# Retention with routed feed-forward on one core: a smaller limit on load traffic in the middle of the kernel, and a weight asked for two loads later

## The chip, the cores and the metric

The kernel runs on one core of one Trainium2 chip. The metric is device time in microseconds (us) of one execution, taken as the median over several. A profiled execution gives a trace: when each engine worked, when each transfer was issued and when it landed. The engines are called by the profile's short names: PE (matrix products; PEld is its loading of stationary operands), DVE (vector), ACT (scalar and activation), POOL (here stores, gathers and some vector work) and SP (here nothing but the issuing of loads).

## The reference, cut to what matters

Two blocks follow each other. The first is a retention layer over 8 batches, 8 heads, 576 positions and head size 64:

```python
scores = scale * np.matmul(q, k.transpose(0, 1, 3, 2))
gamma = 1.0 - 2.0 ** (-5.0 - np.arange(H))
rel = pos[:, None] - pos[None, :]
Dmat = np.where(rel >= 0, gamma[:, None, None] ** rel[None, :, :], 0.0)
ret = scores * Dmat[None, :, :, :]
out = np.matmul(ret, v)
```

Its output, as rows of 512, goes through a mixture-of-depths block. In each batch a score picks 128 of the 576 rows; only these pass a two-layer network, are scaled by a gate and added back:

```python
scores = np.einsum('bsd,d->bs', x, w_gate)
top_idx = np.argpartition(-scores[b], capacity)[:capacity]
h = np.maximum(xe @ w1, 0.0)      # w1 is 512 x 1024
ye = h @ w2                       # w2 is 1024 x 512
out[b, top_idx] = x[b, top_idx] + g[:, None] * ye
```

Everything is float32. The kernel is handed q, k, v and a second copy of k.

## The kernel before, in words

The retention is computed in 36 steps, s = 0 to 35 (`NS` = 36, `NC` = 9 in each of 4 groups of two batches). Step s needs one load, "load s": 1 MB in four quarters of 256 KB, which are q and k with the head dimension on the partitions (quarters 0 and 1) and v and k with the positions on the partitions (2 and 3). Steps 0 to 8 are of a wide kind, 9 and 10 of a kind of their own (`first_step`), 11 to 35 of the "pair" kind. The main loop's pass for step s is called slot s here.

In a slot of the pair kind PE first multiplies q and k (`n_open`, tile `sc_ps`, needs quarters 0 and 1 of load s) in turn with the values' product of the step before (`n_values`, tile `y_ps`). Then come one or two pieces of the feed-forward network of batches chosen earlier (`some`, tiles `h_ps` and `ye_ps`), and then the new state (`n_sums`, tile `u_ps`, needs `vs`) in turn with the states' product of the step before (`n_states`). ACT scales v into `vs` for step s + 1 in the middle of slot s (`scaled`, L238), so it needs quarter 2 of load s + 1 then. POOL stores the finished rows.

All loads are issued by SP, in program order, one after the other. Loads 0 to 14 go as halves of 512 KB (`load`), and are put in SP's queue six slots ahead of their step. The first weight w1 goes as four pieces of 512 KB, two ahead of load 10 and two ahead of load 12. These transfers all pass `transfer` (L105), which makes a new one wait until enough earlier ones have landed: what is under way, itself included, stays at or under `most[0]` = 2048 KB.

Loads 15 to 35 go as quarters of 256 KB, taken from a list `later`. `tick` (L152) takes one from the list; it stands at five places of a slot, four with `AHEAD` = 6 and one with 2. It takes nothing when the next load is further ahead of the slot than that; from load 21 on the limit is 3 slots in place of 6, since loads from 21 on share five buffers (`KEPT`) and the ones before have eight. Each quarter waits for the matrix product at whose place it was asked for, but not for earlier transfers' landing by `most`. The second weight w2 stands in the same list, as eight pieces of 256 KB: four behind load 17, four behind load 18. Its first piece is used in slot 19 (`downs`), its fifth at the end of slot 20.

SP's transfers share eight semaphores in turn (DMAHW0 to DMAHW7), so a transfer can also not start before the eighth one ahead of it has landed.

Of the kernel before, what the change touches and what calls it, by code (L numbers as in the profile page):

```python
# [48 lines left out]
def kernel(  # L49
# [16 lines left out]
    nc = tc.nc  # L66
# [5 lines left out]
    NC = NS // NG  # L72
# [30 lines left out]
    most = [2048]  # L103

    def transfer(out, in_, kb):  # L105
        ins = nc.sync.dma_start(out=out, in_=in_)
        behind.append((ins, kb))
        total = 0
        for n in range(len(behind) - 2, -1, -1):
            total += behind[n][1]  # L110
            if total + kb > most[0]:
                tc.add_manual_dep(ins.ins, behind[n][0].ins.name, LANDED, reason="few at once")
                break

    def room(s):
        if s not in raw:
            pool = loads if s > FEWER or s % (KEPT + LENT) < KEPT else lent
            raw[s] = pool.tile([P, 4, DM], F32, name="raw")

    def load(s, a, go=transfer):  # L120
        room(s)
        go(raw[s][:, 2 * a : 2 * a + 2, :], qkvk[s, a], 512)

    def weight(i, go=transfer):

        w, sb = ((w1, w1_sb), (w2, w2_sb))[i // 4]
        n = w.shape[2]
        flat = sb.rearrange("p h a f -> p (h a f)")
        go(flat[:, n * (i % 4) : n * (i % 4) + n], w[i % 4], 512)


    AHEAD, LED = 6, 14
    pe = {"last": None, "slot": 0}
    later = deque()

# [9 lines left out]

    for s in range(LED + 1, NS):
        later.extend((piece, s, a) for a in (2, 3, 0, 1))
        if s in (LED + 3, LED + 4):
            first = 8 if s == LED + 3 else 12
            later.extend((weight_piece, i) for i in range(first, first + 4))  # L150

    def tick(ahead=AHEAD):  # L152
        if pe["slot"] <= NC or not later:
            return
        s = next(a[1] for a in later if a[0] is piece)
        if s > pe["slot"] + (min(ahead, KEPT - 2) if s > FEWER else ahead):
            return
        f, *a = later.popleft()
        out, in_ = f(*a)
        dma = nc.sync.dma_start(out=out, in_=in_)  # L160
        tc.add_manual_dep(dma.ins, pe["last"].ins.name, LANDED, reason="at its moment")

    def mm(out, w, x, start, stop):
# [3 lines left out]
    n_first = col["eye"]  # L167
    load(0, 0)
    transfer(table[:, :n_first], consts[:, :n_first], 139)
    for a in (2, 3):  # L170
        transfer(*piece(0, a), 256)
# [73 lines left out]
    def w_scores(s):  # L245
        for i in range(2):
            sc_ps[s, i] = bank("sc_ps", "mm" if s == FIRST[1] else "sc")
        first = None
        for j, i, h in wide_heads:
            ins = mm(sc_ps[s, i][:, jt[j]], raw[s][halves[i], 1, jt[j]],  # L250
                     raw[s][halves[i], 0, jt[j]], True, True)
            first = first or ins
        return first
# [100 lines left out]
    def in_turn(a, b, moments):  # L354
        for n in range(H):
            for f in (next(a, None), next(a, None), next(b, None), next(b, None)):
                if f:
                    f()
            if n in moments:
                tick(AHEAD if n == 0 else 2)  # L360
# [563 lines left out]
    for g in range(1, NG):  # L924
        s = NC * g + EARLY[g] + 1
# [4 lines left out]
    s = 2 * NC  # L930
# [23 lines left out]
    s = 3 * NC  # L954
# [23 lines left out]
        plan.setdefault((s, 3), []).insert(0, (some, (1,)))  # L978

    def ahead_of(s):  # L980
        if s <= LED:
            load(s, 1)
            load(s, 0)
        if s in (10, 12):
            weight(s - 10)
            weight(s - 9)
# [7 lines left out]
    def first_step(s):  # L994
        if s == FIRST[0]:
            stored(s - 1)
            opened(s + 1)
        else:
            first_sums()
            n_state(s)  # L1000
            tick()
            stored(s - 1)
        do(s, 1)
        tick()
        do(s, 2)
        w_results(s)
        tick()
        values(s)
        do(s, 3)
        tick()  # L1010
# [3 lines left out]
    for s in range(4, AHEAD):  # L1014
        ahead_of(s)
    scaled(0)
    for s in range(NS + 1):
        pe["slot"] = s
        ahead_of(s + AHEAD)
        if s in FIRST:  # L1020
            first_step(s)
# [3 lines left out]
        if wide:  # L1025
            first = w_scores(s)
# [149 lines left out]
```

## Time and profile before

| What | Value |
|---|---|
| median of 3 executions | 247.94 us (245.8 to 249.35) |
| the profiled execution's own time | 247.39 us |
| its span, first to last instruction | 245.6 us |
| PE busy | 227.7 us, 93% of the span |
| DVE busy | 161.4 us, 66% |
| ACT busy | 105.9 us, 43% |
| POOL busy | 52.8 us, 21% |
| moved by DMA | 56.98 MB, mean 232 GB/s |
| SP's loads | 42.67 MB, 49.8% of 16 DMA engines' span |

The page gives the busy time of each engine, then the span in 40 slices of 6.14 us with the busy share of each in tenths, the granted PE clock in tenths of full speed (PEclk) and the share of the DMA engines. A view of windows gives the same for stretches of choice. A timeline row gives the start in us, the duration, the engine, the line and the tiles, and in brackets how long the engine sat idle just before and what ended that; "issue" there means that nothing in the profile ended it. "DMA to landing" is the time from a transfer's issue to its last byte's arrival. The profiled execution's own time is 1.8 us above its span.

### The profile page before, as it was taken

Reading aid. Unit: us, or ns where it says so; the run is one execution under the profiler, and the core shown is the slowest. Engines: PE = TensorE matmul, PEld = TensorE weight load, DVE = VectorE, ACT = ScalarE, POOL = GpSimd, SP = SyncE. Lnnn points to the kernel's source line nnn. Section 1 sums busy time; section 2 is a strip of 40 time slices with the busy share of each in tenths; the row PEclk is TensorE's granted clock in tenths of the full one; section 3 lists DMA queues with packets and bytes.
Section 4 is the critical chain, followed back from the end, with each engine's and each line's share of the span. In section 5 each row is a group of like instructions: output and inputs, shape, how many; then the busy total and the mean of one; then the engine's idle time right before and its main releaser. Section 6 shows DMA issues by size and latency. Waiting matters only on the chain. (4 is left out here: it accounts for less than half of the span.)

```text
span 245.6 us, 10525 instructions
## 1 busy us (share of the span) xinstructions
PE 227.7 (93%) x4587; PEld 188.2 (77%) x4587; DVE 161.4 (66%) x377; ACT 105.9 (43%) x378; POOL 52.8 (21%) x73
## 2 busy tenths in 40 slices
PE   8799999996985999999998999999999999999991
PEld 6598888985975997656556888888899964499880
DVE  3355979893443558979657469987797987173640
ACT  2456574355462654762725445815572140022100
POOL 1442645520200010011602000220002201310011
PEclk9999999998897999999999999999999999999998
DMA  6989999999998789888996578677511210410002
GB/s 216 370 323 405 329 398 410 397 403 378 364 398 288 234 263 306 280 283 272 281 358 241 169 227 280 201 234 265 180 49 71 105 43 0 131 43 3 0 1 85
DMA packets 22974, 56.98 MB, mean 232 GB/s; under 512 B 2960, under 2 KB 3088, under 8 KB 22928
## 3 DMA queue, kind: packets, MB, share of 16 engines
q1 hardware_dynamic: 18720, 42.67, 49.8%
q0 software_dynamic: 4208, 13.64, 15.3%
q8 instruction: 36, 0.59, 1.0%
q14 instruction: 10, 0.08, 0.1%
HBM read 44.76 MB, written 11.53 MB: 229 GB/s over the span
## 5 line engine op out<-in xcount | busy, mean ns | idle before, releaser
L238 ACT ACTIVATE vs<-raw,table 128x64 f32<-128x64 f32 x192 | 48.4, 338 | 1.3 <-DMA raw<-in_qkvk 1.3
L164 PE MATMUL sc_ps<-raw 64*64 64x64 f32 (+1 forms) x976 | 42.2, 235 | 4.0 <-issue 2.8
L164 PEld LDWEIGHTS sc_ps<-raw 64*64 64x64 f32 (+1 forms) x976 | 37.0, 147 | 10.8 <-issue 8.9
L164 PE MATMUL y_ps<-vs,am 64*64 64x64 f32 (+1 forms) x1152 | 42.6, 224 | 1.3 <-DVE am L272 0.7
L164 PE MATMUL h_ps<-xg,w_sb 128*128 128x128 f32 (+1 forms) x256 | 43.1, 318 | 0.3 <-ACT xg L573 0.2
L164 PEld LDWEIGHTS y_ps<-vs,am 64*64 64x64 f32 (+1 forms) x1152 | 37.7, 138 | 2.9 <-DVE am L272 1.4
L164 PE MATMUL ye_ps<-w_sb,hT 128*128 128x512 f32 (+1 forms) x96 | 39.2, 539 | 0.5 <-DVE o L600 0.5
L418 POOL DMA_DIRECT2D out<-xs x25 | 13.9, 556 | 116.6 <-DVE xs L388 116.6
L164 PEld LDWEIGHTS h_ps<-xg,w_sb 128*128 128x128 f32 x256 | 36.2, 198 | 3.5 <-ACT xg L573 0.5
L164 PE MATMUL u_ps<-vs,raw 64*64 64x64 f32 (+1 forms) x864 | 33.2, 224 | 4.2 <-issue 3.5
L164 PEld LDWEIGHTS u_ps<-vs,raw 64*64 64x64 f32 (+1 forms) x864 | 28.6, 137 | 10.3 <-issue 4.3
L388 DVE TENSOR_TENSOR xs<-y_ps,table 128x512 f32<-128x512 f32 x25 | 17.2, 689 | 28.9 <-PE y_ps L164 28.8
L164 PE MATMUL y_ps<-st,raw 64*64 64x64 f32 x736 | 27.8, 224 | 0.3 <-issue 0.3
L517 DVE SCALAR_TENSOR_TENSOR scr<-row,sc,ahead 128x384 f32<-128x384 f32 (+4 forms) x46 | 26.2, 570 | 2.6 <-ACT row L510 1.4
L399 DVE SCALAR_TENSOR_TENSOR scr<-xs,wg 128x512 f32<-128x512 f32 x36 | 26.1, 726 | 1.0
L164 PEld LDWEIGHTS y_ps<-st,raw 64*64 64x64 f32 x736 | 24.1, 137 | 2.7 <-issue 2.4
L164 PEld LDWEIGHTS ye_ps<-w_sb,hT 128*128 128x128 f32 x96 | 16.8, 189 | 10.4 <-issue 8.2
L272 DVE TENSOR_TENSOR am<-sc_ps,table 128x512 f32<-128x512 f32 x22 | 14.2, 685 | 15.3 <-PE sc_ps L164 15.2
L364 DVE TENSOR_TENSOR am<-sc_ps,table 128x512 f32<-128x512 f32 x25 | 17.2, 688 | 8.5 <-PE y_ps L164 6.8
L378 ACT ACTIVATE xs<-y_ps,table 128x64 f32<-128x64 f32 x72 | 15.8, 332 | 8.2 <-PE y_ps L164 8.1
L370 ACT COPY st<-u_ps 128x512 f32<-128x512 f32 x23 | 13.2, 573 | 13.4 <-PE y_ps L164 10.2
L588 ACT ACTIVATE hT<-h_ps 128x128 f32<-128x128 f32 (+1 forms) x20 | 6.8, 340 | 26.6 <-PE h_ps L164 26.6
(113 smaller groups left out, 265.0 us busy)
## 6 DMA issues: line engine op xcount, KB each, us to landing
raw<-in_qkvk SPq DMA_DIRECT2D x86, 256.0 KB, 4.4
raw<-in_qkvk SPq DMA_DIRECT2D x29, 512.0 KB, 6.4
out<-xs POOLq DMA_DIRECT2D x33, 256.0 KB, 4.9
w_sb<-in_w SPq DMA_DIRECT2D x4, 512.0 KB, 6.7
w_sb<-in_w SPq DMA_DIRECT2D x8, 256.0 KB, 6.0
out<-xs POOLq DMA_DIRECT2D x6, 128.0 KB, 5.4
table<-in_consts SPq DMA_DIRECT2D x1, 314.0 KB
wg<-in_w_gate SPq DMA_DIRECT2D x1, 256.0 KB, 5.0
```

What stands on the lines that cost most here:

```text
L164: pe["last"] = nc.tensor.matmul(out, w, x, start=start, stop=stop, skip_group_check=True)
L238: nc.scalar.activation(out=vs[s][:, hd[h]], in_=raw[s][:, 2, hd[h]], func=AF.Copy, scale=by[:, h : h + 1])
L272: nc.vector.tensor_tensor(out=v(am[s][:, i, :]), in0=v(sc_ps[s, i]), in1=mask.unsqueeze(1).to_broadcast([P, HJ, P]), op=OP.mult)
L364: nc.vector.tensor_tensor(out=heads(am[s][:, 0, :]), in0=heads(sc_ps[s]), in1=caus.unsqueeze(1).to_broadcast([P, H, C]), op=OP.mult)
L370: nc.scalar.copy(out=st[s], in_=u_ps[s // NC])
L378: nc.scalar.activation(out=xs[s][:, hd[h]], in_=y_ps[s][:, at : at + D], func=AF.Copy, scale=decw[:, 1, k, h : h + 1])
L388: nc.vector.tensor_tensor(out=heads(xs[s]), in0=heads(y_ps[s]), in1=dec[:, 1, k, :].unsqueeze(2).to_broadcast([P, H, D]), op=OP.mult)
L399: nc.vector.scalar_tensor_tensor(scr, xs[s], 1.0, wg, op0=OP.mult, op1=OP.mult, accum_out=sc["first" if s in FIRST else g][:, k : k + 1])
L418: nc.gpsimd.dma_start(out=outs[2 * g][k], in_=xs[s])
L517: nc.vector.scalar_tensor_tensor(scr[:, : C * (c1 - c0)], row[g][:, C * c0 : C * c1], sc[g][:, c : c + 1], ahead[:, at + C * c0 : at + C * ...
L588: nc.scalar.activation(out=hT[b // 2, i][:, at : at + n, at0 : at0 + w], in_=t, func=AF.Relu)
```

## The change

Three things change. From load 12 on, `most[0]` is 1280 KB in place of 2048 KB. This is set where load 12 and the two w1 pieces ahead of load 13 are put in the queue, so it holds for load 12, these two pieces, and loads 13 and 14. The quarters that `tick` takes go through `transfer` too as long as the next load in the list is 20 or less; before they did not. The w2 pieces stand behind loads 19 and 20 in place of 17 and 18.

```diff
@@ transfer
                 tc.add_manual_dep(ins.ins, behind[n][0].ins.name, LANDED, reason="few at once")
                 break
+        return ins
@@
-    AHEAD, LED = 6, 14
+    AHEAD, LED, LESS = 6, 14, 20
@@
     for s in range(LED + 1, NS):
         later.extend((piece, s, a) for a in (2, 3, 0, 1))
-        if s in (LED + 3, LED + 4):
-            first = 8 if s == LED + 3 else 12
+        if s in (LED + 5, LED + 6):
+            first = 8 if s == LED + 5 else 12
             later.extend((weight_piece, i) for i in range(first, first + 4))
@@ tick
         out, in_ = f(*a)
-        dma = nc.sync.dma_start(out=out, in_=in_)
+        dma = (transfer(out, in_, 256) if s <= LESS else nc.sync.dma_start(out=out, in_=in_))
         tc.add_manual_dep(dma.ins, pe["last"].ins.name, LANDED, reason="at its moment")
@@ ahead_of
+        if s == NC + 3:
+            most[0] = 1280
         if s <= LED:
             load(s, 1)
             load(s, 0)
```

Only SP's queue moves; the order on PE, ACT, DVE and POOL is the same. The first place is SP's queue at load 12 (`raw_509`), the two w1 pieces, load 13 (`raw_580`) and load 14 (`raw_657`), before:

```order
L106 DMA raw_509<-in_qkvk 128x1024 [waits DMAHW2_49,PE_49,Pool_49]
L106 DMA raw_509<-in_qkvk 128x1024 [waits DMAHW3_49]
L106 DMA w1_sb_73<-in_w1 128x1024 [waits DMAHW4_49]
L106 DMA w1_sb_73<-in_w1 128x1024 [waits DMAHW5_49]
L106 DMA raw_580<-in_qkvk 128x1024 [waits DMAHW6_49,PE_49,Pool_49]
L106 DMA raw_580<-in_qkvk 128x1024 [waits DMAHW7_49]
L106 DMA raw_657<-in_qkvk 128x1024 [waits DMAHW0_49,PE_49,Pool_49]
```

The same place after the change:

```order
L106 DMA raw_509<-in_qkvk 128x1024 [waits DMAHW4_49,PE_49,Pool_49]
L106 DMA raw_509<-in_qkvk 128x1024 [waits DMAHW5_49]
L106 DMA w1_sb_73<-in_w1 128x1024 [waits DMAHW6_49]
L106 DMA w1_sb_73<-in_w1 128x1024 [waits DMAHW7_49]
L106 DMA raw_580<-in_qkvk 128x1024 [waits DMAHW0_49,DMAHW2_49,PE_49,Pool_49]
L106 DMA raw_580<-in_qkvk 128x1024 [waits DMAHW3_49,DMAHW1_49]
L106 DMA raw_657<-in_qkvk 128x1024 [waits DMAHW2_49,PE_49,Pool_49]
```

The semaphores are handed out in turn, and the first `raw_509` transfer itself has number 6. So it waited for the fourth transfer ahead of it and now waits for the second: two halves of 512 KB are under way where four were.

The second place is SP's queue around w2 and load 21. The names' numbers rise along the program, so they also tell in which slot a buffer was asked for. Before, from the end of load 17 (`raw_913`) over load 18 (`raw_1129`):

```order
L160 DMA raw_913<-in_qkvk 128x512 [waits DMAHW1_49,PE_49]
L160 DMA w2_sb_74<-in_w2 128x512 [waits DMAHW2_49,PE_49]
L160 DMA w2_sb_74<-in_w2 128x512 [waits DMAHW3_49,PE_49]
L160 DMA w2_sb_74<-in_w2 128x512 [waits DMAHW4_49,PE_49]
L160 DMA w2_sb_74<-in_w2 128x512 [waits DMAHW5_49,PE_49]
L160 DMA raw_1129<-in_qkvk 128x512 [waits DMAHW6_49,PE_49,Pool_49]
```

After, from the end of load 20 (`raw_1358`) over the second half of w2 to load 21 (`raw_1666`):

```order
L106 DMA raw_1358<-in_qkvk 128x512 [waits DMAHW4_49,PE_49]
L161 DMA w2_sb_74<-in_w2 128x512 [waits PE_49] x3
L161 DMA w2_sb_74<-in_w2 128x512 [waits DMAHW5_49,PE_49]
L161 DMA raw_1666<-in_qkvk 128x512 [waits DMAHW6_49,PE_49,Activation_49]
L161 DMA raw_1666<-in_qkvk 128x512 [waits DMAHW7_49,PE_49]
L161 DMA raw_1666<-in_qkvk 128x512 [waits DMAHW0_49,PE_49]
```

Loads 18, 19 and 20 move ahead of pieces of w2, and the second half of w2 now stands directly ahead of load 21. The four pieces behind load 20 already count as "next is load 21", so `tick` takes them at most 3 slots ahead of step 21: in slot 18. Load 21 follows in slot 19, where it was slot 18, and every later load is one slot later than before too. By the names: before, load 21 is `raw_1563` and load 22 `raw_1671`; after, load 21 is `raw_1666`.

## The prediction

> **What bounds the kernel now.** I read the page first, then PE's busy time in windows, then PE's own timeline at the holes, then the DMA view.
>
> ```profile
> PE 227.7 (93%) x4587; PEld 188.2 (77%) x4587; DVE 161.4 (66%) x377; ACT 105.9 (43%) x378; POOL 52.8 (21%) x73
> q8 instruction: 36, 0.59, 1.0%
> ```
>
> PE is the bound: 17.9 us of the span are left to it. The windows (duration; busy time of PE, PEld, DVE, ACT, POOL; granted PE clock; DMA share; GB/s) show where.
>
> ```profile
> 50.00:55.00 5.00, 5.00 (x133) 4.56 (x130) 4.78 (x17) 2.83 (x11) 1.06 (x2) 1.00 1.01 398
> 55.00:60.00 5.00, 3.11 (x77) 2.79 (x78) 2.27 (x4) 2.68 (x10) 0.00 (x0) 0.96 1.02 385
> 60.00:65.00 5.00, 5.00 (x135) 4.55 (x138) 0.72 (x2) 1.23 (x7) 1.57 (x2) 0.70 0.98 343
> 65.00:70.00 5.00, 4.25 (x109) 3.75 (x102) 2.69 (x6) 3.31 (x13) 0.58 (x1) 1.00 1.04 398
> 70.00:75.00 5.00, 3.26 (x128) 2.93 (x127) 2.00 (x5) 2.53 (x10) 0.56 (x1) 1.00 1.05 396
> 75.00:80.00 5.00, 3.50 (x59) 3.26 (x63) 2.00 (x5) 1.69 (x9) 0.00 (x0) 0.67 0.70 253
> 80.00:85.00 5.00, 5.00 (x181) 4.56 (x174) 2.69 (x6) 3.13 (x13) 0.54 (x1) 0.99 0.75 249
> 85.00:90.00 5.00, 5.00 (x137) 4.62 (x137) 2.08 (x4) 3.25 (x13) 0.54 (x1) 1.00 0.84 249
> 160.00:200.00 40.00, 39.67 (x937) 35.98 (x936) 33.47 (x73) 16.24 (x49) 7.19 (x10) 1.00 0.41 136
> ```
>
> Between 55 and 80 us PE has holes, and twice the clock is cut. Up to 75 us the DMA engines are full (share about 1). Behind 80 us PE is busy nearly throughout, at 160 to 200 us 99%, so what is won before 80 us should reach the end. PE's timeline has the holes:
>
> ```profile
> 58.72 0.21 PE L164 MATMUL u_ps<-vs,raw 64*64 64x64 f32 x1 [1.89 <-issue]
> 70.41 0.27 PE L164 MATMUL u_ps<-vs,raw 64*64 64x64 f32 x2 [1.16 <-issue]
> 76.50 0.27 PE L164 MATMUL sc_ps<-raw 64*64 64x64 f32 x2 [2.83 <-issue]
> ```
>
> All three end with "issue", in the middle of a row of equal products whose operands were there: no wait in the profile explains them. Their distance does. The windows between them:
>
> ```profile
> 58.72:70.41 11.69, 10.53 (x255) 9.51 (x255) 4.07 (x8) 6.23 (x24) 2.15 (x3) 0.85 1.01 369
> 70.41:76.50 6.09, 3.26 (x129) 2.93 (x128) 2.00 (x5) 2.12 (x8) 0.56 (x1) 1.00 1.05 395
> ```
>
> PE and PEld together take 510 instructions between the first two and 257 between the last two: twice, and once, about 256. The page's "instruction" queue carries 36 packets of 0.59 MB, and 9174 PE instructions over 36 packets are 255 each. So PE runs out of instructions: the next packet is late, because it travels behind data. The Trainium skill ("Runtime: NRT & Kernel Launch", section "Instruction fetch mechanics") says that instructions come in 16 KiB blocks of 256, which agrees, and that the cost of crossing a block is mostly hidden, which the three holes contradict.
>
> How late a transfer comes goes with how much is under way. Four answers on "DMA to landing" (minimum, median, maximum): the loads issued at 42.9 to 57 us, at 66.2 to 73.6, at 82 to 107, and the one at 79.5.
>
> ```profile
> DMA to landing us min/median/max: 5.8/6.8/7.2
> DMA to landing us min/median/max: 5.6/6.0/7.2
> DMA to landing us min/median/max: 3.2/3.8/4.1
> DMA to landing us min/median/max: 2.9/2.9/2.9
> ```
>
> A quarter alone takes 2.9 us. With 2048 KB under way 6 to 7 us pass, so 3 to 4 us are queue. At 82 to 107 us, where `tick` paces the loads, 3.8 us pass and PE has no hole.
>
> **The change part by part.** *Gaps two and three* (70.41 and 76.50). Here the quarters and w2 go eight at a time, since the eight semaphores let no more through; "none" was 2048 KB in effect. Now it is five quarters. Nothing slower than 3.8 us is to be expected of them: the estimate is 2.9 alone plus the queue of 1280 in place of 2048 KB, less what passes meanwhile, which puts them next to the 82 to 107 us row. Between 70.41 and 76.50 one block needed 6.09 us with landing at 6.0; at 3.8 its fetch would come 2.2 us sooner, 3.9 us. PE's own work in that block is 3.26 us, so a hole of 0.6 remains of 2.83. The two blocks ahead of it needed 10.53 us of work, 5.3 each, above 3.9: the gap of 1.16 goes. Bounds: with landing at 4.8, as the row for 110 to 131 us has it, the remaining hole is 1.6; with 2.9 it is none.
>
> ```profile
> DMA to landing us min/median/max: 3.1/4.8/7.3
> ```
>
> *The clock behind gap three.* The granted clock of 0.67 at 75 to 80 and 0.99 after it costs (1 - 0.67) x 5 + 0.05 = 1.7 us. The gap of 1.16 us drew no cut (1.00 at 70 to 75), so one of 0.6 should not. Saved so far: 1.16 + 2.2 + 1.7 = 5.1 us.
>
> *Gap one and loads 12 to 14.* The hole of 1.89 us and its cut clock (0.04 x 5 + 0.30 x 5 = 1.7 us) could go too, 3.6 us together. But here loads are needed just as they land:
>
> ```profile
> 57.60 2.02 ACT L238 ACTIVATE vs<-raw,table 128x64 f32<-128x64 f32 x8 [1.30 <-DMA raw<-in_qkvk]
> 61.23 0.37 PE L164 MATMUL sc_ps<-raw 64*64 64x64 f32 x2
> 47.34 2.37 SPq L106 DMA_DIRECT2D w_sb<-in_w  x2
> 50.69 5.77 SPq L106 DMA_DIRECT2D raw<-in_qkvk  x4
> ```
>
> ACT waited 1.30 us for load 13's quarter 2. Slot 13 begins at 61.23; without the hole and the 0.8 us of cut clock up to there it would ask for load 13's second half at 58.5. That half was issued at about 52.5 (second of the four from 50.69) and with a median of 6.8 landed at about 59.2: so even without the hole PE would have waited. And the change slows this very load. Two halves may now be under way in place of four. The w1 pieces at 47.34 and 49.4 waited for load 11's halves (four ahead), so these landed then; from 49.4 on the second halves of load 12, w1 and load 13 follow each other, one landing each. A half of 512 KB takes at least what the very first load took:
>
> ```profile
> DMA to landing us min/median/max: 3.7/3.7/3.7
> ```
>
> The other end is 5.6, the quickest of the full stretch. I take 3.9, the near end plus a little for POOL's stores, since two halves seldom fill the engines: 49.4 + 3 x 3.9 = 61.1 us. Slot 13 then begins where it did before (61.23), after a wait of 2.6 us for data in place of 1.89 for instructions, 0.1 won. That wait is long enough to cut the clock (1.89 was), and all 1.7 us of the cut would then follow it, where 0.9 followed before: 0.8 lost. If the wait falls across two of the clock's intervals there is no cut, and 0.9 is won. I put 0.1 for this part, between -0.7 and +1.0; at the earlier pace (59.2) it would be +2.9.
>
> The quarters of load 15 and on stand in SP's queue behind this. There is room: before, SP issued loads 15 to 17 from 56.57 on, and the `u_ps` row at 70.41 is still slot 14. Five per 3.8 us is a load in 3.0 us, against a slot of 4.85 us (four stores, one a slot, between 86.03 and 105.44). So they stay ahead.
>
> ```profile
> 56.57 8.91 SPq L160 DMA_DIRECT2D raw<-in_qkvk  x12
> ...
> 86.03 0.54 POOL L418 DMA_DIRECT2D out<-xs  x1 [3.81 <-DVE xs L388]
> 105.44 0.54 POOL L418 DMA_DIRECT2D out<-xs  x1 [5.67 <-DVE xs L388]
> ```
>
> *w2 later.* Pieces 1 to 4 are asked for in slot 15 and used in slot 19, pieces 5 to 8 in slot 18 and used at the end of slot 20: two slots, 9.7 us, against landings of 3.8. Free; if not, the feed-forward pieces in PE's queue would hold up the retention behind them.
>
> *Loads 21 to 35 one slot later.* Asked for two slots ahead, the last quarter leaves some 2.5 us into the slot and has 9.7 - 2.5 = 7.2 us to land, against a median of 4.8 and a worst case of 7.3; quarter 2 leaves first and has the middle of the next slot, some 7 us. Mostly covered: 0.2 lost, bounds 0 and 1.
>
> Sum: 1.16 + 2.2 + 1.7 + 0.1 - 0.2 = 5.0 us off the profiled execution's own 247.39: 242.4 us. The runs' median is 247.94, half a microsecond above that execution, well inside their 3.5 us of spread; I leave it out.
>
> **The rivals.** *Loads 12 to 14 keep their pace* (A2): the first gap goes as well, 2.9 in place of 0.1, 239.6 us. For it: the bytes ahead of load 13 are the same, and less runs beside them. Against: 512 KB alone takes 3.7 us, and two per 3.7 us are less than the one per 1.7 us at which they passed before (w1 to load 14: 12 transfers from 37.69 to 56.1).
>
> ```profile
> 37.69 1.79 SPq L106 DMA_DIRECT2D w_sb<-in_w  x2
> ```
>
> *The instruction packet's delay does not hang on what SP has under way* (B). If it waits for its turn among full queues whatever stands in them, gaps two and three stay as long as the DMA engines are full, and w2's departure only moves them: 247.4 - 0.1 + 0.2 = about 247.5 us. Against it: with landing at 3.8 us, DMA was still 0.84 full at 85 to 90 us and PE had no hole. The Trainium skill ("DMA: Bandwidth & Descriptors", section "Queues, rings and completion order") speaks for it: each engine goes round its queue rows a packet at a time, so the instruction row should not stand behind all of SP's bytes. Holes of 1 to 3 us in this trace speak against that, as the whole reason at least.
>
> *The limit starves PE at load 13* (C), the slower side. If a half takes 5.6 us even with two under way, load 13 lands at 49.4 + 3 x 5.6 = 66.2, slot 13 begins 5.0 us later than before and the clock takes 0.8; at such landings gap three keeps 2.4 of its 2.83 us and its cut clock, gap two goes: 5.8 - 1.16 - 0.4 + 0.2 = 4.4 us slower, 251.8. It decides from a landing of about 4.9 us on, where load 13 costs 3.8 and the gaps give 4.0. Against it: 3.8 us for quarters at 82 to 107 us with a megabyte under way.
>
> **How the numbers follow.** The forecast 242.4 has 0.50, A2 (239.6) 0.18, B (247.5) 0.20, C (251.8) 0.12. About 2%, 5.0 us, is what a measurement tells from no change; the line is 243.0, just above the forecast. Its own range is 240.5 to 244.5 by the bounds above, and 0.6 of it lies under the line. Faster by over 2%: 0.30 + 0.18 = 0.48. Slower by over 2% (above 252.9): a third of C, 0.04. Within: 0.48. The range leaves out C and the lower tail of A2: 239.3 to 248.2.
>
> **What would show it.** In the changed kernel's profile: no "issue" hole over 1 us at the 256-instruction borders after slot 14, and a clock of 1.00 at 70 to 80 us; loads at 60 to 80 us landing in about 4 us; in place of the first hole a wait of `sc_ps` on `raw` at slot 13, of 1 to 3 us; DMA share under 1 at 50 to 60 us. Wrong would be: holes that stay although landings fall to 4 us (B), a wait at slot 13 of over 4 us (C), or `vs` or `sc_ps` waiting for `raw` beyond slot 21, which would be the lost slot of lead.

## The result and the profile after

The changed kernel takes 251.91 us (median of 20, 249.4 to 255.79) beside 248.25 us for the kernel before (20, 245.51 to 249.84) on the same chip: a ratio of 1.0124, 95% interval 1.0087 to 1.0161. It is slower, where 2% faster was forecast. Ratios here count only executions within 1.5% of the quickest of their kernel, so that one or two quick executions can shift a ratio by 1% against the medians; executions spread over 2 to 3%, and the median of all stands beside each ratio. The profiled execution of the changed kernel, 249.40 us with a span of 247.6, is the quickest of its 20; so it shows less loss than the median has.

The busy times on the page of the changed kernel are those of before to within 1%; the change moved time, not work. (`transfer`'s new line shifts all that follow: L164 is now L165.)

```profile
PE 229.1 (93%) x4587; PEld 189.1 (76%) x4587; DVE 161.2 (65%) x377; ACT 105.9 (43%) x378; POOL 52.8 (21%) x73
q1 hardware_dynamic: 18720, 42.67, 51.6%
```

The same bytes took 51.6% of the DMA engines' span in place of 49.8%. The windows of the changed kernel, with the columns of the prediction's:

```profile
50.00:55.00 5.00, 5.00 (x120) 4.62 (x119) 4.79 (x15) 2.82 (x11) 1.49 (x3) 1.00 0.95 291
55.00:60.00 5.00, 2.93 (x82) 2.52 (x80) 2.81 (x8) 1.72 (x7) 0.55 (x1) 1.00 0.88 291
60.00:65.00 5.00, 3.40 (x70) 3.29 (x71) 0.69 (x1) 1.26 (x6) 1.02 (x1) 0.61 0.94 320
65.00:70.00 5.00, 5.00 (x141) 4.47 (x139) 2.00 (x5) 2.93 (x11) 0.57 (x1) 0.71 0.91 296
70.00:75.00 5.00, 4.68 (x141) 4.19 (x141) 2.69 (x6) 3.50 (x13) 0.56 (x1) 1.00 0.97 309
75.00:80.00 5.00, 4.40 (x127) 3.94 (x128) 3.85 (x9) 2.81 (x14) 0.54 (x1) 1.00 0.97 336
80.00:85.00 5.00, 4.68 (x128) 4.16 (x127) 2.23 (x6) 3.74 (x15) 0.54 (x1) 1.00 0.95 324
85.00:90.00 5.00, 4.79 (x127) 4.40 (x127) 1.95 (x3) 2.86 (x11) 0.30 (x1) 1.00 0.97 342
90.00:95.00 5.00, 3.75 (x134) 3.30 (x128) 3.78 (x11) 2.50 (x11) 0.53 (x2) 1.00 0.90 300
```

Between 50 and 70 us the DMA engines are 0.88 to 0.95 busy, but move 291 to 320 GB/s where before it was 343 to 398. PE stands idle in the middle of it, and two windows of cut clock follow, (0.39 + 0.29) x 5 = 3.4 us. That sum also counts time in which PE was idle: slot 13 itself has 7.21 us of PE's time here, and 4.4 to 4.7 in the four experiments below that pass it at full clock, so the cut cost some 2.5 to 2.8 us. From 70 us on the clock is full and PE has more done per window than before, until about 80; from there to 95 us it has small holes where before had none. PE's timeline of the changed kernel names them:

```profile
61.60 0.37 PE L165 MATMUL sc_ps<-raw 64*64 64x64 f32 x2 [3.67 <-DMA raw<-in_qkvk]
75.44 0.27 PE L165 MATMUL sc_ps<-raw 64*64 64x64 f32 x2 [0.75 <-issue]
80.14 0.27 PE L165 MATMUL y_ps<-vs,am 64*64 64x64 f32 x2 [0.30 <-issue]
85.21 0.27 PE L165 MATMUL row_ps<-table,sc 64*64 64x64 f32 x2 [0.39 <-issue]
90.41 0.27 PE L165 MATMUL sc_ps<-raw 64*64 64x64 f32 x1 [0.29 <-issue]
95.38 0.38 PE L165 MATMUL h_ps<-xg,w_sb 128*128 128x128 f32 x2 [1.33 <-issue]
```

The first is slot 13 waiting for load 13. All the others stand at the borders of instruction packets: PE and PEld together have 2722, 2977, 3232, 3486 and 3741 instructions on record ahead of them, 254 or 255 apart. Up to 100 us holes and cut clock, by windows in both, come to 6.73 + 3.4 = 10.1 us, where before had 5.88 + 3.4 = 9.3. The slots' starts, read from the timelines of the two kernels (us):

| slot | 12 | 13 | 14 | 15 | 16 | 19 | 24 | 35 |
|---|---|---|---|---|---|---|---|---|
| before | 53.74 | 61.23 | 66.37 | 72.59 | 81.61 | 95.56 | 119.65 | 186.27 |
| after | 53.20 | 61.60 | 68.81 | 73.60 | 79.04 | 96.14 | 122.26 | 188.30 |

At slot 14 the changed kernel is 2.4 us behind, at slot 16 it is 2.6 ahead, at slot 19 it is 0.6 behind and at slot 35 2.0, which is the difference of the spans.

SP's timeline of the changed kernel has the halves one by one. Each waits for the landing of the second one ahead of it:

```profile
49.00 0.33 SPq L106 DMA_DIRECT2D w_sb<-in_w  x1
52.13 0.33 SPq L106 DMA_DIRECT2D w_sb<-in_w  x1
54.33 0.33 SPq L106 DMA_DIRECT2D raw<-in_qkvk  x1
57.12 0.33 SPq L106 DMA_DIRECT2D raw<-in_qkvk  x1
58.55 0.33 SPq L106 DMA_DIRECT2D raw<-in_qkvk  x1
61.57 0.33 SPq L106 DMA_DIRECT2D raw<-in_qkvk  x1
```

So the w1 half issued at 49.00 landed by 54.33, after 5.3 us; the next ones took 5.0, 4.2 and 4.5. The last of these is load 13's second half, landed at 61.57, and PE goes on at 61.60. With four halves under way the median was 6.8: half as much under way shortened the landing by 22 to 38% only, and the pace fell by the rest. It had to fall: even at the 3.7 us of a half alone, two halves at a time (1.05 MB) are 283 GB/s, and SP's queue had moved 318 (3.18 MB in 10 us, below). The DMA view shows the pace, and also why a high DMA share misleads. For 50 to 60 us of the changed kernel:

```profile
DMA packets 844, 2.91 MB, mean 291 GB/s; under 512 B 140, under 2 KB 140, under 8 KB 842
q1 hardware_dynamic: 641, 2.34, 76.7%
```

and for 40 to 50 us of before, when the same kind of halves were under way four at a time:

```profile
DMA packets 1124, 4.03 MB, mean 403 GB/s; under 512 B 146, under 2 KB 146, under 8 KB 1122
q1 hardware_dynamic: 874, 3.18, 80.4%
```

SP's queue took 0.767 x 160 / 2.34 = 52 us of engine time per MB after, and 0.804 x 160 / 3.18 = 40 before, 30% more. This is not a load on the engines that the limit made. The kernel before has the same figure at 85 to 106 us, where no limit holds and `tick` paces the loads, 0.733 x 336 / 4.71 = 52:

```profile
DMA packets 2912, 5.84 MB, mean 278 GB/s; under 512 B 352, under 2 KB 352, under 8 KB 2906
q1 hardware_dynamic: 2584, 4.71, 73.3%
```

So a packet's time on the profile is longer where fewer bytes are under way, and a share of 0.84 to 0.95 does not mean that the engines have nothing left: before moves 249 GB/s at 0.84 (85 to 90 us) and 398 at 1.01 (50 to 55).

### The profile page after: what moved, and what is told of

Read it like the earlier page. It is cut to its first block, busy times and chain, and to the rows that moved or that the text cites. A ratio compares the mean times of both kernels' runs of the same rounds, so it can differ in the third digit from the quotient of the medians.

```text
span 247.6 us, 10524 instructions
## 1 busy us (share of the span) xinstructions
PE 229.1 (93%) x4587; PEld 189.1 (76%) x4587; DVE 161.2 (65%) x377; ACT 105.9 (43%) x378; POOL 52.8 (21%) x73
## 3 DMA queue, kind: packets, MB, share of 16 engines
q1 hardware_dynamic: 18720, 42.67, 51.6%
## 5 line engine op out<-in xcount | busy, mean ns | idle before, releaser
L165 PE MATMUL sc_ps<-raw 64*64 64x64 f32 (+1 forms) x976 | 43.6, 236 | 5.6 <-DMA raw<-in_qkvk 4.2
L165 PEld LDWEIGHTS sc_ps<-raw 64*64 64x64 f32 (+1 forms) x976 | 38.0, 148 | 12.3 <-issue 6.4
L165 PE MATMUL y_ps<-vs,am 64*64 64x64 f32 (+1 forms) x1152 | 43.5, 224 | 1.1 <-DVE am L273 0.7
L165 PE MATMUL h_ps<-xg,w_sb 128*128 128x128 f32 (+1 forms) x256 | 42.6, 315 | 1.6 <-issue 1.3
L165 PEld LDWEIGHTS y_ps<-vs,am 64*64 64x64 f32 (+1 forms) x1152 | 38.3, 138 | 3.2 <-DVE am L273 1.4
L165 PE MATMUL ye_ps<-w_sb,hT 128*128 128x512 f32 (+1 forms) x96 | 39.2, 539 | 0.6 <-DVE o L601 0.6
L165 PEld LDWEIGHTS h_ps<-xg,w_sb 128*128 128x128 f32 x256 | 35.9, 196 | 4.9 <-issue 1.4
L165 PEld LDWEIGHTS u_ps<-vs,raw 64*64 64x64 f32 (+1 forms) x864 | 28.6, 138 | 8.1 <-issue 2.3
L165 PE MATMUL u_ps<-vs,raw 64*64 64x64 f32 (+1 forms) x864 | 33.0, 225 | 0.2 <-POOL vs L235 0.2
L165 PE MATMUL y_ps<-st,raw 64*64 64x64 f32 x736 | 28.2, 225 | 1.8 <-issue 1.7
L400 DVE SCALAR_TENSOR_TENSOR scr<-xs,wg 128x512 f32<-128x512 f32 x36 | 27.2, 755 | 1.0
L165 PEld LDWEIGHTS ye_ps<-w_sb,hT 128*128 128x128 f32 x96 | 16.8, 189 | 11.6 <-issue 9.3
L165 PEld LDWEIGHTS y_ps<-st,raw 64*64 64x64 f32 x736 | 24.4, 138 | 1.4 <-issue 1.0
```

The source lines that it names most:

```text
L165: pe["last"] = nc.tensor.matmul(out, w, x, start=start, stop=stop, skip_group_check=True)
L400: nc.vector.scalar_tensor_tensor(scr, xs[s], 1.0, wg, op0=OP.mult, op1=OP.mult, accum_out=sc["first" if s in FIRST else g][:, k : k + 1])
```

## The experiments

Two theories stood first. P (parts) read the loss off the two traces as a sum: 2.4 us by slot 14 (load 13 late, clock cut), 5.0 won by slot 16, 3.2 lost in slots 17 to 19, and 2 from the lead that loads 21 to 35 lose by w2's later place. W (weight): w2's later place does it all. Two more, T and O, came later and are told where they are tested. None of the kernels leaves out any part of the computation.

**The limit without the move of w2.** The change with w2 left behind loads 17 and 18.

```diff
-        if s in (LED + 5, LED + 6):
-            first = 8 if s == LED + 5 else 12
+        if s in (LED + 3, LED + 4):
+            first = 8 if s == LED + 3 else 12
```

> The limit of 1280 KB as in the change, w2 left behind loads 17 and 18. Theory P (parts): the change's 3.7 us are +2.4 by slot 14 (load 13 late, clock cut), -5.0 up to slot 16 (gaps two and three gone), +3.2 in slots 17 to 19 (the backlog of loads, carried more slowly, keeps the instruction packets late for longer) and +2 in slots 21 to 25 (loads 21 to 35 one slot later, by w2's place). Alone, the limit keeps the first three: +0.6 us on before, ratio 1.000 to 1.006. Theory W (w2's place does it all): the limit alone gains what was forecast, 0.980.

Measured: 251.76 us (6 executions, 248.44 to 255.76) beside 247.62, ratio 1.0107 (1.0023 to 1.019). The loss is there without w2's move, so W falls. P's sum falls too: it had 0.6 us of loss without w2's move, and the medians have 4.1. PE's timeline of this kernel, whose profiled execution (251.99 us) is near its median:

```profile
63.82 0.37 PE L165 MATMUL sc_ps<-raw 64*64 64x64 f32 x2 [4.31 <-DMA raw<-in_qkvk]
```

**The move of w2 alone.** Before, with w2 behind loads 19 and 20.

```diff
-        if s in (LED + 3, LED + 4):
-            first = 8 if s == LED + 3 else 12
+        if s in (LED + 5, LED + 6):
+            first = 8 if s == LED + 5 else 12
```

> w2 behind loads 19 and 20, no limit beyond before's 2048 KB. Theory P: only the lost slot of lead remains, +1 to +2 us, 1.004 to 1.008; the hole at 70 us stays, the one at 76 us stays or moves, since the engines are as full. Theory W: the whole loss, 1.012 or more, and more than the change itself has, as the limit's gain is missing.

Measured: 245.83 us (6, one of them far out at 739.93) beside 247.62, ratio 0.9892 (0.9805 to 0.9979). P had expected it to be slower, 1.004 to 1.008, and it is not; whether it is a gain is asked again below.

**The limit on the halves alone.** One line added to before, so that only load 12, two w1 pieces and loads 13 and 14 are held.

```diff
     def ahead_of(s):
+        if s == NC + 3:
+            most[0] = 1280
```

> 1280 KB for the halves alone (load 12, two w1 pieces, loads 13 and 14); quarters and w2 as before. Theory P: the wait of 3 to 4 us at slot 13 and the cut clock come as in the change, +2.4 us by slot 14, and gaps two and three stay, so 1.010. Rival: the wait only takes the place of the first hole and the later ones shrink since SP is further behind: 1.000.

Measured: 252.55 us (6, 250.46 to 256.2) beside 247.62, ratio 1.02 (1.0135 to 1.0265), twice what P had expected. The halves' limit alone costs as much as the whole change, or more. The timeline of its PE, the windows and SP's timeline; the profiled execution was the slowest of its six (256.2 us), so the rows show the mechanism, not its usual size:

```profile
63.72 0.37 PE L164 MATMUL sc_ps<-raw 64*64 64x64 f32 x2 [4.33 <-DMA raw<-in_qkvk]
```

```profile
60.00:65.00 5.00, 1.28 (x48) 1.28 (x52) 0.00 (x0) 2.70 (x11) 0.24 (x1) 0.64 0.87 292
65.00:70.00 5.00, 5.00 (x108) 4.55 (x100) 1.52 (x3) 2.26 (x10) 0.78 (x1) 0.67 0.94 294
```

```profile
47.32 1.73 SPq L106 DMA_DIRECT2D raw<-in_qkvk  x2
51.79 3.18 SPq L106 DMA_DIRECT2D w_sb<-in_w  x2
57.61 6.41 SPq L106 DMA_DIRECT2D raw<-in_qkvk  x4
```

Load 13 leaves SP at 57.61 where it left at 50.69 before. The same wait and the same two windows of cut clock are there as in the changed kernel. (Here and in the kernel without w2's move slot 12 had waited for its load as well, 1.51 and 0.95 us.)

**The limit on the quarters alone.** The change with w2 in its old place and the limit set only after load 14.

```diff
-        if s == NC + 3:
-            most[0] = 1280
         if s <= LED:
             load(s, 1)
             load(s, 0)
+        if s == LED:
+            most[0] = 1280
```

> 1280 KB for the quarters of loads 15 to 20 and w2 (behind loads 17 and 18) alone; halves as before at 2048 KB. Theory P: load 13 as before, gaps two and three smaller (-5.0), later small holes at the 256-instruction borders up to 95 us (+2 to +3): 0.988 to 0.996. Rival, that the late holes eat all of it: 1.000.

Measured: 248.05 us (12 executions) beside 247.62, ratio 0.9988 (0.994 to 1.0036). No gain, as the rival had it. The waits of its PE between 50 and 100 us (total, times, longest):

```profile
PE u_ps L165 <- issue: 2.4, 2, 1.3
PE y_ps L165 <- issue: 2.2, 2, 1.9
PE sc_ps L165 <- issue: 1.2, 1, 1.2
PE h_ps L165 <- issue: 1.1, 1, 1.1
PE row_ps L165 <- issue: 0.7, 1, 0.7
```

Seven smaller holes of 7.5 us in all, up to 94 us, stand in place of before's three of 5.88; the clock is not cut (1.00 in all windows from 55 to 95), which is worth up to 3.4 us against before's profile, and still the time is the same. Its loads issued between 60 and 90 us take 4.8 us to land, by the median:

```profile
DMA to landing us min/median/max: 3.8/4.8/6.2
```

So the limit on the quarters spreads the delay over more borders instead of taking it away. This execution is 0.5 us ahead of before's at slot 19 (95.06 for 95.56), level at slot 24 and behind from a hole of 1.41 at 123.99 on.

**The move of w2 with the lead kept.** The kernel with only w2 moved, and besides `tick` takes a w2 piece one slot earlier, so that loads 21 to 35 keep their lead of 3.

```diff
+        if later[0][0] is weight_piece:
+            s -= 1
```

> x2_weight_alone with w2's pieces counted to the load that they stand behind, so that its second half is asked for in slot 17 and loads 21 to 35 keep their 3 slots of lead. x2 gave 0.989. If the lost slot of lead costs something, this is below x2, 0.980 to 0.986; if loads two slots ahead are on time, as I forecast, it is the same, 0.987 to 0.991.

Measured: 246.58 us (12) beside 248.41, ratio 1.0041 (0.9981 to 1.0102). The median is 0.7% lower and the ratio above 1, so nothing can be told; the expected 0.987 to 0.991 did not come. The same kernel once more, with other executions of before:

> The kernel of x6 once more, for its size alone. Its median was 0.7% under before's there, x2's (the same without the kept lead) 0.7%, x12's (with more under way) 0.6%, each with an interval that reaches or nearly reaches 1. If w2's later place is worth something by itself: median 0.4 to 1.0% under before's, 245.5 to 247.0 us. If the three were luck: within 0.3%.

Measured: 248.67 us (12, two of them far out at 433.18 and 739.95) beside 247.35, ratio 1.0007 (0.9939 to 1.0074). The two medians lie on either side of before's. Neither the lead nor w2's place moves the time by an amount that can be told from none. The 1% of the move alone was most likely luck; that kernel was not run again.

**Three halves under way.** Theory T (throughput) said that the pace falls with every half less under way; O (order), that the order of what is under way decides and not the amount, so that three cost nothing. The halves' limit alone, at three:

```diff
     def ahead_of(s):
+        if s == NC + 3:
+            most[0] = 1536
```

> The halves' limit at 1536 KB, three under way; the rest as before. With 1280 KB (two under way) load 13 came 3 to 4 us late and the ratio was 1.020. Theory T (few transfers under way leave the engines' fixed time uncovered, so throughput falls with each one less): about a third to a half of it, 1.005 to 1.010, with a wait at slot 13 of 1 to 2 us. Theory O (the order of what is under way, not the amount, decides): no loss, 1.000.

Measured: 246.99 us (6) beside 248.41, ratio 1.011 (1.0011 to 1.0209); median and ratio disagree in sign. Slot 13 starts at 58.99 without a wait of PE for data, and SP issues load 13 when it did before (50.59, there 50.69). PE's and SP's timelines and the windows:

```profile
58.99 0.27 PE L164 MATMUL sc_ps<-raw 64*64 64x64 f32 x1
50.59 6.65 SPq L106 DMA_DIRECT2D raw<-in_qkvk  x4
```

```profile
50.00:55.00 5.00, 5.00 (x124) 4.56 (x119) 4.79 (x15) 2.82 (x11) 1.66 (x4) 1.00 0.99 360
55.00:60.00 5.00, 4.35 (x147) 3.88 (x145) 3.07 (x8) 2.98 (x12) 0.60 (x2) 1.00 0.89 332
```

With 360 and 332 GB/s it moves less than before there (398 and 385) and more than the change (291), which is T's throughput; but load 13 is on time, so T's wait of 1 to 2 us does not come, and the time leaves the rest open. That order and not amount decides, as O has it, is not shown by this.

**The whole change with three.** The deciding one: `most[0] = 1536` in place of 1280, all else as changed.

```diff
         if s == NC + 3:
-            most[0] = 1280
+            most[0] = 1536
```

> The whole change with 1536 KB in place of 1280: three halves or six quarters under way. x7 (1536 on the halves alone) had no wait for data at slot 13 and a median 0.6% under before's; x3 (1280) was 2% over. If the change's loss is the two halves under way, it is gone: median within 1% of before's, 246 to 250 us, and no wait of sc_ps for raw at slot 13. If six quarters or w2's place cost too, 250 to 252.

Measured: 248.0 us (11) beside 247.71, ratio 1.0003 (0.9954 to 1.0052). The loss of the change is gone, and nothing is won. Its slot 13 waits a quarter as long as in the changed kernel, where none had been expected, and slot 14 has a wait of another kind:

```profile
59.32 0.28 PE L165 MATMUL sc_ps<-raw 64*64 64x64 f32 x2 [0.89 <-DMA raw<-in_qkvk]
PE xg_ps L572 <- DMA xr<-out,idx: 1.5, 1, 1.5
```

The second is PE waiting for POOL's gather of the chosen rows. Three experiments have it, those that begin slot 14 early: this one (63.74, wait 1.46), the three halves alone (64.27, 1.02) and the next experiment (64.55, 1.14); before (66.37) does not. The row gives the total, the times and the longest. So of what is won at load 13 a part is lost again at once, which the prediction did not reckon with. This kernel is still 1.2 us ahead of before at slot 19 (94.35 for 95.56), and loses it to late holes of 2.10 us at 119.29 and 1.13 at 124.93.

**Quarters limited, w2 late, lead kept.** The change with the limit set only after load 14, and the lead kept:

```diff
+        if later[0][0] is weight_piece:
+            s -= 1
...
-        if s == NC + 3:
-            most[0] = 1280
...
+        if s == LED:
+            most[0] = 1280
```

> The change without its two costs as the runs so far have them: limit of 1280 KB on the quarters alone, w2 behind loads 19 and 20, lead of 3 slots kept. x4 (quarters' limit alone) gave 0.999 and x2 (w2 alone) 0.989. If the two add up: 0.985 to 0.990. If the limit takes away what w2's place gives, because it stretches the backlog: 0.995 to 1.000.

Measured: 248.92 us (6) beside 248.41, ratio 1.0146 (1.0025 to 1.0266); neither expectation covers it. No gain from the three parts that are left when the halves run free.

**More under way.** The kernel with w2 late and the lead kept, with 3072 KB for loads 12 to 14:

```diff
     def ahead_of(s):
+        if s == NC + 3:
+            most[0] = 3072
```

> x6 (w2 behind loads 19 and 20, lead kept, no new limit) with more under way in place of less: 3072 KB for the halves from load 12 on, six of them. If throughput at loads 12 to 14 still rises with what is under way, load 13 lands earlier and slot 13 begins up to 1 us sooner: 0.985. If four are enough to fill the engines, nothing but more queue ahead of the instruction packets: 0.993 to 1.000.

Measured: 246.12 us (12) beside 247.71, ratio 0.9962 (0.9921 to 1.0003). The median is 0.6% lower, but the interval reaches no change. Slot 13 begins at 59.80, inside the 58.95 to 61.23 of the kernels with four halves, so nothing is won there by six.

**Are the holes late packets of instructions?** The prediction rests on it. More instructions ahead shift every border: the holes should keep their number in PE's stream and move in the work. First 64 more small products of zeros at the start (69 in place of 5):

```diff
-    warmed(256, 256, 256, 256, P)
+    t = bank("warm_ps")
+    for n in range(69):
+        mm(t[:C, :C], zeros[:C, :C], zeros[:C, :C], True, True)
```

> The kernel before with 69 small products of zeros in place of 5 larger ones at the start, while PE waits for the first load: 128 PE and PEld instructions more, no transfer changed. If PE's holes that end with issue are late packets of 256 instructions, each hole stands 128 instructions away from where it stood in the work (none at the same product of u_ps or sc_ps as before), and the counts of PE and PEld instructions from the start to the holes stay multiples of 256 apart from one another and from before's holes. If something in the work itself stops PE there (an operand, a PSUM bank), the holes stay at the same products. Time: within 1% of before, since holes are moved, not removed.

Measured: 255.92 us (4) beside 248.41, ratio 1.0488 (1.0346 to 1.063). The expected 1% was missed because PE comes to the first product of the retention only at 16.1 us, behind the products of zeros, where before starts it at 5.2. It tells nothing of the borders: a float32 product is two instructions of PE and two of PEld, so 64 more are just one packet of 256, and the holes came at the same products. With 21 products in place of 5, 64 instructions more:

> x5 again with a shift that is no whole block. A product of float32 stands as two PE and two PEld instructions in the trace, so x5's 64 products more were 256 instructions, one block exactly, and its holes could not move in the work. Here 21 small products stand in place of 5, 64 instructions more. Late instruction packets: the holes that end with issue keep their count from the start (about 1985, 2497, 2754, with PE and PEld together) and so stand 64 instructions, 16 products, earlier in the work than before. A cause in the work: they keep their products, and their count is 64 higher.

Measured: 249.12 us (3) beside 247.71, ratio 1.0101 (1.0039 to 1.0164). PE's timeline of it has three holes up to 71 us:

```profile
58.19 0.21 PE L164 MATMUL u_ps<-vs,raw 64*64 64x64 f32 x1 [0.55 <-issue]
64.38 0.21 PE L164 MATMUL y_ps<-vs,am 64*64 64x64 f32 x1 [2.70 <-issue]
70.95 0.27 PE L164 MATMUL y_ps<-vs,am 64*64 64x64 f32 x1 [2.18 <-issue]
```

Windows from the start to each hole count the instructions (the numbers behind x, of PE and PEld):

```profile
0.00:58.18 58.18, 55.67 (x978) 49.69 (x979) 38.00 (x91) 28.97 (x112) 23.23 (x33) 1.00 0.97 371
0.00:64.37 64.37, 59.17 (x1106) 52.83 (x1107) 40.30 (x94) 31.18 (x120) 24.81 (x35) 1.00 0.98 374
0.00:70.94 70.94, 63.56 (x1234) 56.70 (x1234) 42.30 (x99) 34.00 (x131) 25.38 (x36) 1.00 0.99 375
```

and those of before, to its first and second hole:

```profile
0.00:58.71 58.71, 52.97 (x978) 46.55 (x979) 39.49 (x92) 29.56 (x114) 23.01 (x33) 1.00 0.96 363
0.00:70.40 70.40, 63.50 (x1233) 56.06 (x1234) 43.56 (x100) 35.78 (x137) 25.16 (x36) 0.98 0.97 364
```

The first hole comes after 978 + 979 = 1957 instructions in both, though 64 of these are other instructions; the third of the one and the second of the other after 2468 and 2467; the steps are 256. (The counts in the expectation were some 30 too high, for before as well.) The holes belong to the packets, not to the work. That a packet is late because it stands behind data is not tested by this. For it speaks that before's three holes begin in windows that move 385 to 398 GB/s, and that none of over 0.3 us comes at 249 to 292 GB/s (80 to 110 us). Against it, as the whole reason, speak a hole of 2.50 us in this last kernel at 90.22, at 305 GB/s, and the 1.38 us at 110.60 of the changed kernel, at 259. (The page of the Trainium skill that the prediction named, "Runtime: NRT & Kernel Launch", section "Instruction fetch mechanics", has the block of 256 right; that its crossing is mostly hidden does not hold here, where it costs 0.55 to 2.70 us three times in 13 us.)

## Why the prediction was wrong

**Gap one and loads 12 to 14: the step that failed.** Its landing of 3.9 us for a half with two under way took the nearest row to be that of a load alone (3.7). Measured: 5.3, 5.0, 4.2 and 4.5, a mean of 4.75, and a pace of 291 GB/s in all. The reason given for the 3.9, that two halves seldom fill the engines, did not make the landings quick: they took 4.2 to 5.3 us although the pace was far under the 403 GB/s that the engines had moved. That load 13 came at 61.57 and not far from the forecast 61.1 is two errors that cancel: from load 12's second half to load 13's there were three landings of 4.9, not 3.9 (2.9 us more), but the first of them began at 46.96 and not at 49.4, most likely since load 11 had less beside it. PE's wait was 3.67 for a forecast 2.6, and the cut clock, by windows, 3.4 us for 1.7.

The offset was wrong as well. The forecast let the new wait take the place of a hole of 1.89 us with its cut clock. That hole is the longest of six: the executions with the same loads up to here (before, w2 alone, quarters alone, w2 late with the lead kept twice, and the quarters with both) have holes of 1.89, 0.76, 1.29, 1.75, 0.83 and 1.66 us there and start slot 14 at 66.37, 64.84, 64.86, 66.39, 65.32 and 64.55, a mean of 65.4. Only the two longest were followed by a cut clock. The three with halves held to 1280 (the change, limit without w2, halves alone) start it at 68.81, 70.01 and 70.08, a mean of 69.6. That is 4.2 us late, for a forecast gain of 0.1; the halves' limit alone measured 4.9 us in the medians, the whole change 3.7.

**Gaps two and three: the packets right, the landing wrong.** Instructions do come late, the holes shrank (1.16 gone, 2.83 to 0.75), and the clock at 70 to 80 us is 1.00 as forecast. From slot 14 to slot 16 the changed kernel needs 79.04 - 68.81 = 10.2 us where before needed 81.61 - 66.37 = 15.2: 5.0 us less, as much as this term's 5.1: 1.16 us of hole in slot 14, and in slot 15 2.08 of hole and 1.50 of PE's time at the cut clock. But the landing did not fall to 3.8 us; that the holes shrank as forecast with landings of 4.9 is luck in the size, since the bound for 4.8 had left a hole of 1.6. The loads and w2 pieces of the changed kernel under the limit, from 70 us on:

```profile
DMA to landing us min/median/max: 4.7/4.9/5.1
```

The 3.8 came from a stretch where `tick` paced the loads and little stood in the queue. Here SP issued against the limit until 88 us and the rest of w2 until 93, the DMA share stayed at 0.90 to 0.97 with 300 to 342 GB/s, and the borders behind 80 us, free of holes before, got 0.30, 0.39, 0.29 and 1.33: 2.3 us of the 5.1. The step that PE is busy behind 80 us, so that what is won before should reach the end, held the work of 80 to 95 us for fixed, while the change put the remaining traffic just there. With the halves free, the limit on the quarters measures 0.9988: no part of the term that could be measured reaches the end. Of the 3.2 us lost between slots 16 and 19 the holes are 2.3 and 0.9 is not explained. The further 1.4 between slots 19 and 35 has a hole of 1.38 at 110.60 in it and was seen in one execution. Such late holes (1.41 at 123.99 with the quarters limited, 2.10 at 119.29 with three halves, 1.94 at 120.95 with only w2 moved) come and go with and without the limit, and no run here says when.

The named signs came mixed: DMA share under 1 at 50 to 60 us and a full clock at 70 to 80 as said; a wait at slot 13 of 3.67, between the 1 to 3 of the forecast and the 4 of C; landings of 4.9 for 4; and a hole over 1 us after slot 14, at 95.38.

**w2 later, and the lost lead: right.** Forecast 0 and 0.2 us; no difference measured. The named sign did come: for load 23, ACT's `vs` waits for its quarter in the changed kernel, and PE's timeline has no wait for data behind it.

```profile
111.30 0.82 ACT L239 ACTIVATE vs<-raw,table 128x64 f32<-128x64 f32 x3 [1.39 <-DMA raw<-in_qkvk]
```

**The rivals.** C, with 0.12, had the place, the direction and, at 251.8 us, the time (251.91). Its point of decision, a landing of 4.9 us, was about met by the measured 4.75. Its parts were not, so the time was partly luck: it had landings of 5.6, slot 13 beginning 5.0 us later and the third hole nearly whole, while slot 13 began 0.4 us later (61.60 for 61.23), the cut clock was twice as long by windows, the third hole shrank to 0.75, and there were new holes behind 80 us. B, that the limit doesn't help the packets, was right in what the time shows of the quarters, though not in its reason: the holes did change. The argument held against B, no hole at a DMA share of 0.84, took the share for fullness; those 5 us moved 249 GB/s. A2 fell. The range, up to 248.2, left C out; the evidence against C was again the 3.8 us of a paced stretch, the same row that carried the gain.

## What to carry to other kernels

A limit on what is under way buys shorter landings only as far as the queue was longer than the engines could use; below that it takes bytes per second, and a load that is needed as it lands shows it at once. Before setting one, divide the bytes that it allows by the landing of one transfer alone: if that is under the pace now, the limit slows the loads whatever else it does. Take the landing under a limit from a stretch in which the issuer runs against a limit, not from one where little is asked for. And when the same bytes are only spread out, look at what the later stretch had free: here the delays of the instruction packets went along with the traffic.

## What the runs showed of the hardware

Two halves of 512 KB under way (with POOL's stores beside) kept the DMA engines 0.88 to 0.95 busy but moved only 291 GB/s; four moved up to 403, and six, at 50 to 60 us, 412. Three were between, 360 and 332 at 50 to 60 us, and cost the whole change no measurable time.

The DMA share is no measure of what the engines could still move. SP's queue shows 40 us of engine time per MB with four or six halves under way, 44 with three (alone, at 50 to 60 us), 48 with five quarters (70 to 90 us of the change), and 52 with two halves, but 52 as well where no limit holds and loads come at their own pace (before, 85 to 106 us). Why a packet's time grows when less is under way was not found.

An instruction packet that comes late costs up to 2.83 us of PE in before and 3.1 with the halves alone held to 1280 KB, and each float32 product of 64 x 64 counts four instructions towards the next border.
